# A planned mLSTM and feed-forward kernel: the last 64 rows of w_in in two slices of their own, the gates of chunk 0 in a first small load, and own due times for single jobs

## The chip, the core and the metric

The program runs on one core of a Trainium2 chip. The time is the device time of one execution in microseconds (us). The median of three runs of the kernel before is 493.52 us, the lowest 492.1 and the highest 497.03.

## What is computed

An mLSTM (a recurrent attention with exponential gates) over 4 batches, 8 heads, 768 steps and head width 40, and then a feed-forward layer over all 3072 tokens, all in float32. Cut to what matters:

```python
for t in range(768):
    m_new = maximum(f[t] + m, i[t])
    C = exp(f[t] + m - m_new) * C + exp(i[t] - m_new) * outer(v[t], k[t])
    n = exp(f[t] + m - m_new) * n + exp(i[t] - m_new) * k[t]
    y[t] = sigmoid(o[t]) * (C @ q[t]) / maximum(abs(n @ q[t]), 1)
    m = m_new
x = y as (3072 tokens, 320)
h = x @ w_in                      # 320 x 2048
g = h * clip(h + 3, 0, 6) / 6
out = g @ w_out                   # 2048 x 320
```

## The kernel before

The sequence is cut into chunks of 128 steps. A unit is three chunks of one batch (384 tokens), and there are eight units. Each unit has two tasks (four heads each), so task 2u and 2u+1 belong to unit u; within a task there is one job of each kind per chunk, and names such as `gw2_2` read task 2, chunk 2. `gates` scans the two gates along time on 32 partitions and turns the results into columns by products on the tensor engine (tile `pc`, which needs the loads `img` and `signs`). `gate` makes the decay matrix `gw`: for the first eight by products on the tensor engine (`gb`), later by a broadcast DMA of a scratch array (`gw<-gsc`), a masking instruction on POOL and four exponentials on ACT. `front` multiplies keys and queries (`s`) and DVE multiplies the result into `gw`; `state` and `all_states` make and update the state (`c`, `C`); `back` multiplies by the values (`o`) and gives back the `gw` buffer in the first tasks; `fin` divides, applies the output gate and transposes into `xh` and `xl` (tile `x`).

The feed-forward layer keeps float32 accuracy by splitting each operand into a high and a low part. For block f of 128 of the 2048 hidden columns, `mm1` runs eight products into `h` (L907): three with the first 128 rows of w_in, three with the next 128, and two with the last 64 rows, whose high and low parts lie one above the other in the tile `wtl`. ACT and DVE then make `g` (L921, L923), its high part `gh` (L407) and low part `gl` (L931); `mm2` accumulates three products per block into `acc` (L950 to L952). Two `h` tiles exist, so the third `mm1` of a unit waits until DVE has read the first.

The weights come as raw words that two passes on ACT (L839, L841), two on DVE (L844, L849) and splits (`whi`, `wlo`, `wtl` for w_in; `vh`, `vl` for w_out) turn into these parts. w_in comes in eight slices of 640 words a partition (`weight_slice`, kind `i`: 512 words of the first 256 rows, and 128 of the last 64), w_out in eight of 640. Three `raw` buffers hold them: a load waits until DVE has run L849 on an earlier slice.

Nothing is ordered by the hardware's own choice. A planner in the kernel (`Plan`) takes jobs as generators with due times and estimated costs, and writes one fixed order for PE, ACT, DVE, POOL and the DMA queue of SP. Each engine then works through its row strictly in order, so an instruction that waits holds back all behind it on that engine, and a DMA that waits for its buffer holds back all later DMAs. While the tensor engine has nothing ready in the first unit, the planner sets filler products (`pw`, L428) that keep it active; they end with the first `mm1`. Of 182 fillers, 59 stand ahead of the first product of `gates` and 123 behind it.

## Time and profile before

| | us |
|---|---|
| median of three runs | 493.52 |
| lowest, highest | 492.1, 497.03 |
| the profiled execution, its own time | 497.03 |
| its span, first to last instruction | 495.3 |
| PE busy in the span | 483.8 |
| DVE, ACT, POOL busy | 364.2, 304.9, 43.7 |

The profile shows one execution, the one of 497.03 us; 1.7 us of it lie outside its span. In its rows each line is a group or an instruction with its start, its length and, in square brackets, the idle time of its engine just before it and what ended that. Matmuls overlap their successors, so a group on PE ends about 0.2 us after the next one starts, and the start of the next row is the better mark. PEclk or the clock column is the granted clock of the tensor engine, 1.00 at 2.4 GHz and 0.50 at 1.2 GHz.

### The profile page before, as it was taken

Reading aid. Unit: us, or ns where it says so; the run is one execution under the profiler, and the core shown is the slowest. Engines: PE = TensorE matmul, PEld = TensorE weight load, DVE = VectorE, ACT = ScalarE, POOL = GpSimd, SP = SyncE. Lnnn points to the kernel's source line nnn. Section 1 sums busy time; section 2 is a strip of 40 time slices with the busy share of each in tenths; the row PEclk is TensorE's granted clock in tenths of the full one; section 3 lists DMA queues with packets and bytes.
Section 4 is the critical chain, followed back from the end, with each engine's and each line's share of the span. In section 5 each row is a group of like instructions: output and inputs, shape, how many; then the busy total and the mean of one; then the engine's idle time right before and its main releaser. Section 6 shows DMA issues by size and latency. Waiting matters only on the chain.

```text
span 495.3 us, 10928 instructions
## 1 busy us (share of the span) xinstructions
PE 483.8 (98%) x4222; PEld 465.8 (94%) x4222; DVE 364.2 (74%) x828; ACT 304.9 (62%) x766; POOL 43.7 (9%) x65
## 2 busy tenths in 40 slices
PE   7999998999999999999999999999999999999997
PEld 7899898989999999998899999999999999999997
DVE  4789997999859789597668779688767887534431
ACT  3787997976666657376564656566654755434331
POOL 2012212021210100010010001001010000000000
PEclk9799999999999999999999999999999999999999
DMA  8565948323422323132412423114320110000001
GB/s 269 195 230 197 328 159 299 100 106 119 135 62 65 124 91 106 58 108 80 141 48 66 143 72 119 45 54 156 124 65 22 63 49 15 0 1 26 15 1 41
DMA packets 24676, 50.74 MB, mean 102 GB/s; under 512 B 2576, under 2 KB 9168, under 8 KB 24624
## 3 DMA queue, kind: packets, MB, share of 16 engines
q1 hardware_dynamic: 24624, 50.05, 30.9%
q8 instruction: 33, 0.54, 0.4%
q14 instruction: 19, 0.16, 0.1%
HBM read 46.01 MB, written 4.03 MB: 101 GB/s over the span
## 4 chain that ended last, share of the span: by engine, by line
PE 68%; DVE 12%; DMA 10%; ACT 5%; issue 2%; POOL 2%; SPq 0%; POOLq 0%; DVEq 0%; ACTq 0%
PE h L907 27%; PE acc L950 9%; PE acc L951 8%; PE acc L952 8%; DMA gw<-gsc 7%; PE s L705 4%; PE s L708 2%; ACT gw L678 2%; POOL gw L672 2%; DVE gl L931 2%; PE o L756 2%; DVE g L923 1%; PE c L606 1%; DMA nat<-in_nat_dram 1%; DVE p L738 1%
## 5 line engine op out<-in xcount | busy, mean ns | idle before, releaser
L950 PE MATMUL acc<-vh,gh 128*128 128x320 f32 x384 | 121.0, 315 | 0.0
L951 PE MATMUL acc<-vl,gh 128*128 128x320 f32 x384 | 118.3, 308 | 0.0
L952 PE MATMUL acc<-vh,gl 128*128 128x320 f32 x384 | 118.2, 308 | 0.0
L923 DVE SCALAR_TENSOR_TENSOR g<-g,h 128x384 f32<-128x384 f32 x128 | 67.7, 550 | 55.4 <-ACT g L921 54.5
L907 PE MATMUL h<-xh,whi 128*128 128x384 f32 x256 | 90.8, 355 | 2.4 <-DVE g L923 2.2
L921 ACT ACTIVATE g<-h,half 128x384 f32<-128x384 f32 x128 | 69.9, 575 | 34.1 <-PE h L907 33.4
L907 PE MATMUL h<-xh,wlo 128*128 128x384 f32 x256 | 86.3, 337 | 0.0
L907 PE MATMUL h<-xl,whi 128*128 128x384 f32 x256 | 86.2, 337 | 0.0
L678 ACT ACTIVATE gw<-gw,cT 128x128 f32<-128x128 f32 x160 | 54.1, 397 | 44.4 <-POOL gw L672 44.4
L931 DVE TENSOR_TENSOR gl<-g,gh 128x384 fp32r<-128x384 f32 x128 | 70.7, 567 | 4.8 <-ACT gh L407 3.6
L407 ACT CAST gh<-g 128x384 fp32r<-128x384 f32 x128 | 63.1, 514 | 16.0 <-DVE g L923 15.5
L950 PEld LDWEIGHTS acc<-vh,gh 128*128 128x128 f32 x384 | 72.0, 188 | 0.5
L951 PEld LDWEIGHTS acc<-vl,gh 128*128 128x128 f32 x384 | 72.2, 188 | 0.0
L952 PEld LDWEIGHTS acc<-vh,gl 128*128 128x128 f32 x384 | 72.0, 188 | 0.0
L672 POOL TENSOR_SCALAR_AFFINE_SELECT gw<-gw 128x512 f32<-128x512 f32 x40 | 29.3, 733 | 300.3 <-DMA gw<-gsc 228.9
L907 PEld LDWEIGHTS h<-xh,whi 128*128 128x128 f32 x256 | 48.0, 188 | 5.7 <-DVE g L923 4.1
L907 PEld LDWEIGHTS h<-xh,wlo 128*128 128x128 f32 x256 | 48.0, 188 | 0.3 <-DVE wlo L865 0.3
L907 PEld LDWEIGHTS h<-xl,whi 128*128 128x128 f32 x256 | 48.1, 188 | 0.0
L713 DVE TENSOR_TENSOR gw<-s,gw 128x512 f32<-128x512 f32 x48 | 33.0, 687 | 18.0 <-PE s L708 9.1
L907 PE MATMUL h<-xl,wtl 128*128 128x384 f32 x128 | 43.1, 337 | 0.0
L907 PE MATMUL h<-xh,wtl 128*128 128x384 f32 x128 | 43.1, 337 | 0.0
L722 ACT ACTIVATE ht<-s,eG 128x42 f32<-128x42 f32 x120 | 25.5, 296 | 25.4 <-DVE gw L713 25.4
(97 smaller groups left out, 789.9 us busy)
## 6 DMA issues: line engine op xcount, KB each, us to landing
st<-in_qk_dram SPq DMA_DIRECT2D x48, 256.0 KB, 4.0
gw<-gsc SPq DMA_DIRECT2D x40, 256.0 KB, 3.3
nat<-in_nat_dram SPq DMA_DIRECT2D x16, 492.0 KB, 4.9
rawi<-in_w_in_dram SPq DMA_DIRECT2D x8, 640.0 KB, 6.0
rawo<-in_w_out_dram SPq DMA_DIRECT2D x8, 640.0 KB, 6.0
on<-in_on_dram SPq DMA_DIRECT2D x8, 480.0 KB, 4.5
out_dram<-ob SPq DMA_DIRECT2D x24, 160.0 KB, 2.3
f_s<-in_fg_dram SPq DMA_DIRECT2D x1, 96.0 KB, 4.1
```

Of the source, the lines that this page charges most:

```text
L407: nc.scalar.copy(dst, src)
L672: nc.gpsimd.affine_select(gw, gw, pattern=[[0, 4], [1, L]], compare_op=ALU.is_ge, fill=NEG, base=0, channel_multiplier=-1)
L678: nc.scalar.activation(gw[:, h, :], src[:, h, :], AF.Exp, bias=cT[:, c, r0 + h : r0 + h + 1], scale=1.0)
L713: nc.vector.tensor_tensor(gw.rearrange("p (z j) l -> p z (j l)", z=2), sp[:, :, : 2 * L], gw.rearrange("p (z j) l -> p z (j l)", z=2), ALU ...
L722: nc.scalar.activation(hv[:, z, j], sp[:, z, 2 * L + j * E2 : 2 * L + j * E2 + E2], AF.Copy, scale=eG[:, c, r0 + h : r0 + h + 1])
L907: nc.tensor.matmul(hp, w, x, start=n == 0, stop=n == len(seq) - 1)
L921: nc.scalar.activation(g, hp, AF.Relu, bias=half, scale=1.0 / 6.0)
L923: nc.vector.scalar_tensor_tensor(g, g, 1.0, hp, ALU.min, ALU.mult)
L931: E(e).tensor_sub(gl, g, gh.bitcast(F32))
L950: nc.tensor.matmul(acc, gh[:, ts_], VH[f // 4][:, f % 4, :], start=f == 0, stop=False)
L951: nc.tensor.matmul(acc, gh[:, ts_], VL[p][:, f % 2, :], start=False, stop=False)
L952: nc.tensor.matmul(acc, gl[:, ts_], VH[f // 4][:, f % 4, :], start=False, stop=f == NF - 1)
```

## The change

Four things are changed.

1. w_in comes as eight slices of 512 words (its first 256 rows) and two new slices of kind `t`, of 512 words each, that hold the last 64 rows: half of the 2048 columns in each, on all 128 partitions. A `t` slice takes the same four passes as the others, then two casts and two subtractions of 64 partitions by 512 on ACT or DVE, in place of two casts and two subtractions of 64 by 128 in each of the eight slices. `mm1` for block f waits for `i` slice f//2 and `t` slice f//8.
2. Both gates lie side by side in one input, `figs`. Chunk 0 of both comes in a first load (32 KB), the other five chunks in a second (160 KB); the copy for `img` and the `signs` come by two loads that are a request of their own to the planner.
3. The planner adds a number to the due time of single jobs (`SHIFT`, some 120 entries between -44.6 and +43.2, such as -44.6 for `weight_slice_t_0_0`, -35.9 for `weight_slice_i_7_14`, +24.1 for `weight_slice_i_2_4`).
4. Its other constants are set anew, and so are letters that give passes to engines (`ENGINES`): `ht<-s,eG` is now always on DVE (30 of 40 were on ACT), the first cast of `p` always on ACT and the second on either (56 of 72 casts are on ACT now, 36 before), `weigh` may go to ACT too, and the last subtraction of `vb` and a multiplication of the output gate may go to POOL.

A second way to make `wlo`, by products on PE (`NPE`), is in the code and switched off (`NPE = 0`).

```diff
+NPE = 0
-ENGINES = 'ddpxadxxdaddddddxdaaaaadaaxxy'
+ENGINES = 'dxpxadzxdaadddddxxyaaaadaaxxd'
...
     def add(self, due, gen, after=(), att=1, slack=None, hot=False):
         self.n += 1
+        due += SHIFT.get(name_of(gen), 0.0)
...
         if c0 == 0:
-            yield "q", 200, 1.9
-            nc.sync.dma_start(f_s, fg)
-            nc.sync.dma_start(i_s, ig)
-            nc.sync.dma_start(img[:BH], ig)
+            both = figs.rearrange("p (k t) -> p k t", k=2)
+            yield "q", 200, 0.95
+            nc.sync.dma_start(GT["fi"][mid, :, :L], both[:, :, :L])
+            nc.sync.dma_start(GT["fi"][mid, :, L:], both[:, :, L:])
+            t = plan.now["t"]
+            yield "q", 200, 0.95
+            nc.sync.dma_start(img[:BH], figs[:, S:])
             nc.sync.dma_start(signs, ident_d[:, 128:])
+            event("signs")
+            plan.now["t"] = t
...
         yield "wait", "ident"
+        yield "wait", "signs"
...
+        m = WC if kind == "o" else WI
-        yield "q", 655
-        nc.sync.dma_start(raw.rearrange("p n w -> p (n w)"), (w_in if kind == "i" else w_out)[i].bitcast(U32))
+        yield "q", 1.024 * m
+        nc.sync.dma_start(raw.rearrange("p n w -> p (n w)"), {"i": w_in, "t": w_tail, "o": w_out}[kind][i].bitcast(U32))
...
-            e = yield pick(4, a=0.6, d=Lock(0.55))
-            cast(e, tl[a, 0:128], w[a, 512:640])
-            cast(e, tl[z, 128:256], w[z, 512:640])
-            e = yield pick(5, d=Lock(0.64), g=2 * cg(128))
-            E(e).tensor_sub(tl[z, 0:128], w[a, 512:640], tl[a, 0:128].bitcast(F32))
-            E(e).tensor_sub(tl[a, 128:256], w[z, 512:640], tl[z, 128:256].bitcast(F32))
...
+        elif kind == "t":
+            a, z = slice(0, 64), slice(64, 128)
+            ta, tz = wtl[:, i * 1024 : i * 1024 + WI], wtl[:, i * 1024 + WI : (i + 1) * 1024]
+            for p, o, tl in ((a, z, ta), (z, a, tz)):
+                e = yield pick(4, a=0.18 + 0.00084 * WI, d=lf(WI))
+                cast(e, tl[p], w[p])
+                e = yield pick(5, d=ld(WI), g=cg(WI))
+                E(e).tensor_sub(tl[o], w[p], tl[p].bitcast(F32))
...
     for n in range(WS):
         plan.add(moe_at(0, n / WS) - WAI, weight_slice("i", n, 2 * n))
+        if n % 4 == 0:
+            plan.add(moe_at(0, n / WS) - WAI + WAT, weight_slice("t", n // 4, 2 * n))
```

The order that the planner writes moves at many places. Three of them follow; line numbers of the changed kernel are higher by 10 to 34.

The DMA queue of SP at the start of the program, before (`on` is the output gate, `nat` keys and values, `st` keys and queries, `rawi` a slice of w_in):

```order
L553 DMA on_105<-in_on_dram 128x3x320
L446 DMA f_s<-in_fg_dram 32x768
L447 DMA i_s<-in_ig_dram 32x768
L448 DMA img<-in_ig_dram 32x768
L449 DMA signs<-in_ident_dram 128x192
L436 DMA ident<-in_ident_dram 128x128
L542 DMA nat_106<-in_nat_dram 128x984
L529 DMA st_0_107<-in_qk_dram 128x512
L833 DMA rawi_109<-in_w_in_dram 128x1280
```

The same place in the change (`rawt` is a slice of the last 64 rows):

```order
L447 DMA ident<-in_ident_dram 128x128
L575 DMA on_105<-in_on_dram 128x3x320
L459 DMA fi<-in_figs_dram 32x2x128
L460 DMA fi<-in_figs_dram 32x2x640
L551 DMA st_0_106<-in_qk_dram 128x512
L564 DMA nat_107<-in_nat_dram 128x984
L856 DMA rawt_109<-in_w_tail_dram 128x1024
L463 DMA img<-in_figs_dram 32x768
L464 DMA signs<-in_ident_dram 128x192
```

`signs` moves from fifth to ninth, behind `st`, `nat` and the first `t` slice. On PE the first `s` product now stands ahead of the first product of `gates`; of 173 fillers 107 stand ahead of that product (40 of them behind the `s`), and 66 behind it.

DVE ahead of the last product of unit 0's stretch, the multiplication into `gw2_2`, before (`vr`, `vl` belong to w_out, `yi`, `yo` to the raw passes):

```order
L849 SCALAR_TENSOR_TENSOR vr1_630<-yo1_542,rawo1_481 128x640
L819 TENSOR_TENSOR xl0_529<-x1_1_0_751,xh0_528 128x384
L766 TENSOR_TENSOR ht2_595<-ht2_595,o2_1_770 128x168
L844 TENSOR_SCALAR yi4_627<-yi4_627 128x640
L877 TENSOR_TENSOR vl1_781<-vr1_630,vh0_616 128x640
L713 TENSOR_TENSOR gw2_2_625<-s2_2_771,gw2_2_625 128x512
L819 TENSOR_TENSOR xl0_529<-x2_1_0_786,xh0_528 128x384
```

The same place in the change:

```order
L867 TENSOR_SCALAR yi4_614<-yi4_614 128x512
L841 TENSOR_TENSOR xl0_535<-x1_1_0_735,xh0_534 128x384
L871 SCALAR_TENSOR_TENSOR vr1_757<-yo1_560,rawo1_523 128x640
L735 TENSOR_TENSOR gw2_2_657<-s2_2_746,gw2_2_657 128x512
L788 TENSOR_TENSOR ht2_628<-ht2_628,o2_1_750 128x168
L746 TENSOR_TENSOR ht2_628<-s2_2_746,eG_82 128x168
L911 TENSOR_TENSOR vl1_781<-vr1_757,vh0_607 128x640
L841 TENSOR_TENSOR xl0_535<-x2_1_0_772,xh0_534 128x384
```

The low part of the second slice of w_out (`vl1`) moves from just ahead of that multiplication to behind it. On PE, the `front` products of the next task (`s3_0`) move from behind the first two `mm1` to ahead of them, and the first three `mm1` then follow each other.

ACT around the first `mm1`, before (`g0_0` is the first pass over the first `h`):

```order
L678 ACTIVATE gw3_0_746<-gw3_0_746,cT_81 128x128 x4
L678 ACTIVATE gw3_1_778<-gw3_1_778,cT_81 128x128 x2
L921 ACTIVATE g0_0_879<-h0_0_849,half_80 128x384
L678 ACTIVATE gw3_1_778<-gw3_1_778,cT_81 128x128
L407 CAST vh1_892<-vr2_888 128x640
L921 ACTIVATE g0_1_904<-h0_1_878,half_80 128x384
```

The same place in the change:

```order
L700 ACTIVATE gw3_0_732<-gw3_0_732,cT_81 128x128 x4
L417 CAST whi_75<-yi4_614 128x2x256
L862 ACTIVATE yi5_794<-rawi5_782 128x512
L864 ACTIVATE rawi5_782<-rawi5_782 128x512
L955 ACTIVATE g0_0_864<-h0_0_840,half_80 128x384
L577 ACTIVATE on1_800<-on1_800 128x3x320
L955 ACTIVATE g0_1_882<-h0_1_863,half_80 128x384
```

The two passes over the raw words of w_in slice 5 now stand ahead of `g0_0`, and the output gate of unit 1 ahead of `g0_1`. The load of slice 5 waits for the buffer that `vr1` (the DVE rows above) gives back.

## Rows read from the trace of the kernel before

**Rows 1.** From the page: the span, the busy time of each engine, and the clock of the tensor engine in 40 slices of the span.

```profile
span 495.3 us, 10928 instructions
PE 483.8 (98%) x4222; PEld 465.8 (94%) x4222; DVE 364.2 (74%) x828; ACT 304.9 (62%) x766; POOL 43.7 (9%) x65
PEclk9799999999999999999999999999999999999999
```

**Rows 2.** The timeline of PE from 0 to 62 us: start, length, instruction, and in brackets the idle time before it.

```profile
1.06 5.37 PE L428 MATMUL pw<-ones 128*128 128x128 bf16 x59 [1.06 <-POOL ones L421]
7.97 0.49 PE L491 MATMUL pc<-signs,img 96*128 96x128 f32 x2 [1.55 <-DVE img L472]
...
9.42 0.71 PE L705 MATMUL s<-st 64*128 64x128 f32 x8 [0.23 <-DMA st<-in_qk_dram]
10.07 0.34 PE L428 MATMUL pw<-ones 128*128 128x128 bf16 x3
...
16.06 0.44 PE L606 MATMUL c<-vp,nat 128*64 128x42 f32 x8 [0.26 <-ACT gw L678]
...
17.86 0.44 PE L606 MATMUL c<-vp,nat 128*64 128x42 f32 x8 [0.34 <-DVE C L409]
...
41.41 1.12 PE L428 MATMUL pw<-ones 128*128 128x128 bf16 x17
...
43.09 1.63 PE L428 MATMUL pw<-ones 128*128 128x128 bf16 x26
...
52.23 1.09 PE L756 MATMUL o<-nat,gw 128*128 128x42 f32 x8 [0.94 <-DVE gw L713]
53.15 0.42 PE L907 MATMUL h<-xh,whi 128*128 128x384 f32 x1
```

**Rows 3.** Stretches of 2 us from 8 to 18 us: us, busy time of PE, weight loads, DVE, ACT and POOL with their instructions, the granted clock, the share of the DMA engines, and GB/s.

```profile
8.00:10.00 2.00, 1.77 (x22) 1.54 (x22) 1.87 (x5) 0.52 (x4) 0.00 (x0) 1.00 0.98 379
...
14.00:16.00 2.00, 1.80 (x18) 1.59 (x16) 1.89 (x6) 1.47 (x8) 0.08 (x1) 1.00 0.94 370
16.00:18.00 2.00, 1.60 (x21) 1.46 (x23) 1.94 (x7) 1.96 (x9) 0.00 (x0) 1.00 0.10 38
```

**Rows 4.** One wider stretch, all engines in the same columns.

```profile
18.50:25.50 7.00, 7.00 (x54) 6.43 (x54) 3.87 (x13) 4.09 (x11) 0.00 (x0) 0.52 0.39 131
```

**Rows 5.** Waits of PE from 53 to 120 us: total, times, longest.

```profile
PE h L907 <- DVE g L923: 2.0, 2, 1.4
```

**Rows 6.** The same from 120 us to the end.

```profile
PE o L758 <- DVE C L619: 0.8, 2, 0.5
PE o L761 <- DVE p L738: 0.5, 1, 0.5
PE o L760 <- ACT p L407: 0.3, 1, 0.3
PE h L907 <- DVE g L923: 0.2, 1, 0.2
```

**Rows 7.** The DMA queue of SP at the start: start, length of the issue, tile.

```profile
3.05 0.42 SPq L449 DMA_DIRECT2D signs<-in_ident_dram  x1
...
5.12 0.86 SPq L833 DMA_DIRECT2D rawi<-in_w_in_dram  x2
```

**Rows 8.** The timeline of ACT: the instruction that waited for the first slice of w_in.

```profile
11.00 0.79 ACT L839 ACTIVATE yi<-rawi 128x640 f32<-128x640 f32 x1 [1.07 <-DMA rawi<-in_w_in_dram]
```

**Rows 9.** The chain of waits of the whole program, around the first `mm1`: start, length, what the end waited for.

```profile
40.49 5.72 DMA gw<-gsc
...
46.36 0.64 POOL gw L672
...
47.03 0.69 ACT gw L678 x2
...
50.31 1.04 issue
...
51.50 0.69 DVE gw L713
52.23 1.09 PE o L756 x8
53.32 2.86 PE h L907 x16
```

**Rows 10.** The timeline of DVE: one instruction of the same stretch.

```profile
50.27 1.30 DVE L877 TENSOR_TENSOR vl<-vr,vh 128x640 fp32r<-128x640 f32 x1
```

**Rows 11.** The view of the tile `rawi`: time from issue to landing of its eight loads.

```profile
DMA to landing us min/median/max: 3.8/6.0/9.3
```

**Rows 12.** Groups of ACT instructions from 53 to 120 us: count, busy us, mean ns of one, and the idle time before them.

```profile
L722 ACT ACTIVATE ht<-s,eG 128x42 f32<-128x42 f32 x17 | 3.7, 298 | 0.4 <-DVE gw L713 0.4
L407 ACT CAST whi<-yi 128x512 fp32r<-128x512 f32 x4 | 2.5, 620 | 0.0
...
L407 ACT CAST wtl<-yi 64x128 fp32r<-64x128 f32 x8 | 2.4, 297 | 0.1
L841 ACT ACTIVATE rawi<-rawi 128x640 uint32<-128x640 uint32 x3 | 2.4, 791 | 0.0
```

**Rows 13.** From the page, the costliest groups: the passes that turn `h` into `g`, with count, busy us, mean ns of one, and the idle time of the engine before them.

```profile
L923 DVE SCALAR_TENSOR_TENSOR g<-g,h 128x384 f32<-128x384 f32 x128 | 67.7, 550 | 55.4 <-ACT g L921 54.5
...
L921 ACT ACTIVATE g<-h,half 128x384 f32<-128x384 f32 x128 | 69.9, 575 | 34.1 <-PE h L907 33.4
```

**Rows 14.** One stretch later on, in the columns of rows 3.

```profile
80.00:100.00 20.00, 18.59 (x158) 17.43 (x157) 17.70 (x40) 19.54 (x42) 1.56 (x4) 1.00 0.58 202
```

More of the change, by code (lines that the diff above doesn't have):

```diff
@@ L25 @@
 WC = 640
+WI = 512
+WAT = 14.426
 NEG = -1.0e30
@@ L49 @@
 NRAW = 3
-SPAN = 85.078
-T0 = 227.472
-AH = 11.606
+SPAN = 82.689
+T0 = 235.691
+AH = 6.112
 GP = [1, 2, 1, 2]
-G0 = -164.7
-G1 = 19.632
-G2 = 100.338
-AH1 = 3.428
+G0 = -140.122
+G1 = 29.702
+G2 = 118.356
+AH1 = 8.351
 FC = 0
 FCS = {2: [[(0, 2)], [(0, 1), (1, 1)]], 3: [[(0, 3)], [(0, 2), (2, 1)], [(0, 1), (1, 1), (2, 1)], [(0, 1), (1, 2)]], 1: [[(0, 1)], [(0, 1)]]}
-LON = -24.316
-WAI = -16.391
-WAO = -37.306
-WAS = 137.753
-MV = -2.634
-DELTA = -1.049
+LON = -28.143
+WAI = -13.123
+WAO = -40.095
+WAS = 109.704
+MV = -2.298
+DELTA = -1.405
 EGW = 1
-EV = 80.942
-EG = -23.479
+EV = 102.156
+EG = -38.496
 HOP = 0.167
@@ L82 @@
 RATE_D = 300.0
-BL = 3.335
+BL = 2.337
 T_WARM = 6.9
 WGAP = 0.055
-ENGINES = 'ddpxadxxdaddddddxdaaaaadaaxxy'
-BG = -0.356
-BA = -1.135
-BD = -0.41
+ENGINES = 'dxpxadzxdaadddddxxyaaaadaaxxd'
+BG = -0.283
+BA = -0.362
+BD = -0.296
 GS = 6
 FD = 2
-FIN0 = -213.18
+FIN0 = -202.157
 NE = 0
@@ L148, in mat, with name_of @@
     return m
+def name_of(gen):
+    code, given = gen.gi_code, gen.gi_frame.f_locals
+    return "_".join([gen.__name__] + [str(given[v]) for v in code.co_varnames[: code.co_argcount]])
 class Plan:
@@ L349, in mlstm_moe_kernel @@
 @with_exitstack
-def mlstm_moe_kernel(ctx: ExitStack, tc: tile.TileContext, ig, fg, qkd, natd, ond, w_in, w_out, ident_d, out):
+def mlstm_moe_kernel(ctx: ExitStack, tc: tile.TileContext, figs, qkd, natd, ond, w_in, w_tail, w_out, ident_d, out):
     nc = tc.nc
@@ L430, in mlstm_moe_kernel @@
     GT = {k: early["ea"].tile(sh, F32, name=k) for k, sh in dict(
-        f_s=[64, S], i_s=[64, S], lf=[64, S], img=[128, S], signs=[128, 192], one=[64, L], sel=[128, 8, L]).items()}
+        fi=[64, 2, S], lf=[64, S], img=[128, S], signs=[128, 192], one=[64, L], sel=[128, 8, L]).items()}
     GT.update({k: early["ea"].tile([128, L], BF16, name=k) for k in ("mask", "identb")})
+    GT["nident"] = early["ea"].tile([128, L], F32R, name="nident")
     def load_ident():
@@ L851, in weight_slice @@
         if kind == "i":
-            hi, lo, tl = whi[:, :, fs], wlo[:, :, fs], wtl[:, fs]
-            wm = w[:, 0:512].rearrange("p (a f) -> p a f", a=2)
-            a, z = slice(0, 64), slice(64, 128)
+            fs = slice(i * 256, (i + 1) * 256)
+            hi, lo = whi[:, :, fs], wlo[:, :, fs]
+            wm = w.rearrange("p (a f) -> p a f", a=2)
             e = yield pcast(24, 512)
             cast(e, hi, wm)
-            plan.now["t"] -= ca(512)
-            e = yield pick(4, a=0.6, d=Lock(0.55))
-            cast(e, tl[a, 0:128], w[a, 512:640])
-            cast(e, tl[z, 128:256], w[z, 512:640])
-            e = yield pick(5, d=Lock(0.64), g=2 * cg(128))
-            E(e).tensor_sub(tl[z, 0:128], w[a, 512:640], tl[a, 0:128].bitcast(F32))
-            E(e).tensor_sub(tl[a, 128:256], w[z, 512:640], tl[z, 128:256].bitcast(F32))
-            e = yield psub(7, 512)
-            E(e).tensor_sub(lo, wm, hi.bitcast(F32))
+            if i < NPE:
+                yield "wait", "nident"
+                gb = yield ("get",) + banks(0, "o")
+                pb = bank(gb, [128, 2, 256], f"wl{i}")
+                yield "p", mat(1, 512, 4) + mat(1, 512)
+                nc.tensor.matmul(pb, ident, wm, start=True, stop=False)
+                nc.tensor.matmul(pb, GT["nident"], hi, start=False, stop=True)
+                yield "a", ca(512)
+                nc.scalar.copy(lo, pb)
+                put(*gb)
+            else:
+                e = yield psub(7, 512)
+                E(e).tensor_sub(lo, wm, hi.bitcast(F32))
+        elif kind == "t":
[6 more added lines that the diff above has]
+                E(e).tensor_sub(tl[o], w[p], tl[p].bitcast(F32))
         put(*gy)
@@ L997, in mlstm_moe_kernel @@
         if quad == 0:
[L998 removed]
+            plan.add(max(due(u, k - 1 + LON), -98.0), load_on(u), (), 1, sl)
         before = {cp: "{}_{}".format(*order[rank[task, cp] - 1]) if rank[task, cp] else None for cp in range(n)}
@@ L1040, in mlstm_moe_kernel @@
             plan.add(0, release(rel_vp), states)
-    plan.add(0, release(open_moe), [f"gw{t}_{x}" for t, x in order[2 * UNITS[0] : GB]] + [f"fin1_{UNITS[0]-1}", f"state0_{UNITS[0]-1}", f"state1_{UNITS[0]-1}"])
+    plan.add(0, release(open_moe), [f"gw{t}_{x}" for t, x in order[2 * UNITS[0] : GB]] + [f"wi{n}" for n in range(NPE)] + [f"fin1_{UNITS[0]-1}", f"state0_{UNITS[0]-1}", f"state1_{UNITS[0]-1}"])
     for n in range(WS):
         plan.add(moe_at(0, n / WS) - WAI, weight_slice("i", n, 2 * n))
+        if n % 4 == 0:
+            plan.add(moe_at(0, n / WS) - WAI + WAT, weight_slice("t", n // 4, 2 * n))
         plan.add(moe_at(0, n / WS) - WAO + SPAN / 16, weight_slice("o", n, 2 * n + 1))
@@ L1048, in mlstm_moe_kernel @@
             pre = [f"m1_{u}_{f-1}"] if f else [f"m1_{u-1}_{NF-1}"] * (u > 0)
-            plan.add(moe_at(u, f / NF) - MV, mm1(u, f), pre + [f"wi{f//2}", f"fin{2*u+1}_{UNITS[u]-1}", "mo"], 0)
+            plan.add(moe_at(u, f / NF) - MV, mm1(u, f), pre + [f"wi{f//2}", f"wt{f//8}", f"fin{2*u+1}_{UNITS[u]-1}", "mo"], 0)
         for p in range(NF // 2):
@@ L1056, in mlstm_moe_kernel @@
         plan.run()
-_INS = ["ig", "fg", "qk", "nat", "on", "w_in", "w_out", "ident"]
+_INS = ["figs", "qk", "nat", "on", "w_in", "w_tail", "w_out", "ident"]
 _OUTS = [((B * S, DM), "float32")]
```

41 lines of the change are left out of this document (22 added, 19 removed).

## The prediction

> **What bounds the kernel now.** I began with busy times. The tensor engine is busy for 483.8 of 495.3 us at nearly full clock throughout; DVE and ACT have a quarter and a third of the span to spare [rows 1]. The change takes no real product away and adds none, so it can alter only four things: when the first real product starts, how many fillers stand among the real ones, how long PE waits, and at which clock the real ones run.
>
> The second view was the timeline of PE up to the first `mm1`, which starts at 53.15 us [rows 2]. Ahead of the first product of `gates` at 7.97 us stand 59 fillers and a wait of 1.55 us for a scan on DVE. Behind it, four waits add up to 0.23 + 0.26 + 0.34 + 0.94 = 1.77 us, and 123 fillers lie between the real products. The third view was the clock by stretches: it is full up to 18 us and half from about 18.5 to 25.5 us [rows 3, 4]. Seven us at half clock cost some 3.4 us of the tensor engine's time (7.00 busy us at 0.52: 7.00 x 0.48). The fourth was the list of waits after 53 us: 2.0 us up to 120 us [rows 5], 0.8 + 0.5 + 0.3 + 0.2 = 1.8 us later [rows 6], some 3.8 us in all. So all that the change can win back is in the first 53 us, bar those 3.8 us.
>
> The profiled execution took 497.03 us, the longest of the three shown; the median is 493.52, 3.5 us below it. That is about the price of the half-clock stretch. I read the other runs as having less of it, which no row shows.
>
> **The start.** `signs` was issued at 3.05 us as the fifth load [rows 7]; now it is the ninth, and the first product of `gates` needs it. The ninth load of before is the first slice of w_in, issued at 5.12 us; ACT waited for it until 11.00 us [rows 7, 8]. Nine loads then carried 480 + 4 x 96 + 64 + 492 + 256 + 640 = 2316 KB (the sizes of the tiles in the order). Now they carry 64 + 480 + 32 + 160 + 256 + 492 + 512 + 96 + 96 = 2188 KB. The queue moved 370 to 379 GB/s in those stretches [rows 3], so 128 KB less is some 0.35 us: a landing at about 10.6 us, against 7.97 us for the product before. That is +2.6 us. One real group, `s` of chunk 0, which took 10.07 - 9.42 = 0.65 us [rows 2], now runs in that time. Net **+2.0 us**; bounds +1.4 (the 40 fillers behind that `s` end by about 10.0 us, and the load is no later) and +3.0 (landing a us later). The smaller first gate load, which lets the scan start earlier, gains nothing here: the scan is no longer what ends last. It only brings the scans of later chunks forward.
>
> **The fillers.** Behind the first gate product stand 66 in place of 123. One costs (1.63 - 1.12) / (26 - 17) = 0.057 us at full clock [rows 2]. 57 fewer are **-3.2 us**, if real products are ready in their place; if not, each turns into a wait and the gain is nothing.
>
> **The waits up to the first mm1s.** The stretch behind `o1_2` (40.4 us) is set by a chain: the `gw` load of 5.72 us, the mask, the exponentials, a multiplication on DVE at 51.50 us [rows 9]. In that chain DVE lost time to `vl1`, which took 1.30 us [rows 10] after waiting for ACT and now stands behind the multiplication. So about 1.3 us of chain go, and the PE work behind `o1_2` is about as long as the chain that is left; I expect some 0.7 us of wait there, as against 0.94. A second wait is likely early on: DVE now does the `t` slice among the scans before the first `gw` is multiplied, some 0.8 us for `o0_0`. The third is new. On ACT the two passes over slice 5 now stand ahead of `g0_0`, and the third `mm1` can't start before DVE has finished `g0_0`. Their load waits for a buffer that DVE gives back just ahead of the multiplication into `gw2_2`. From there to the first `mm1` go that multiplication (0.69 [rows 9]), `o2_2` (53.15 - 52.23 = 0.92 [rows 2]) and `s3_0` (about 1.0 by its place in the order: the `s` of 0.65 and a smaller one), 2.6 us. A load takes at least 3.8 us [rows 11], 0.35 less for 128 KB, so it lands 0.85 us behind the start of the first `mm1`. Two passes of about 0.63 us (0.791 x 512/640 [rows 12]) and `g0_0` on ACT and DVE (0.575 + 0.55 [rows 13]) end at 3.25 us, 3.9 with the DVE passes of slices 2 and 5 in between; the first two `mm1` cover 2.86 [rows 9]. That leaves about 1.1 us of wait. In sum 0.8 + 0.7 + 1.1 = 2.6 us in place of 1.77: **+0.8 us**. Bounds: -1.8 (nothing waits) and +6.3 (that load takes 9.3 us, the longest of rows 11, so 5.5 more than the shortest).
>
> **The clock.** The fall at about 18.5 us came after 14 to 18 us with PE busy for 1.80 + 1.60 of 4 us, and with no single wait over 0.34 us since 9.5 us [rows 2, 3]. In the change the same small products (`c`, `o`, `pc`) stand in that stretch, with the wait for `o0_0`. I therefore leave the clock as it was, 0.0 us, with bounds -3.4 (no such stretch) and +3.4 (a second one). The Trainium skill, TensorE: Matmul & The Clock Gate, section on HAM oscillation, has the clock fall when the engine idles long between bursts, as in a wait for a DMA. By it this stretch should not have come at all, and the sum would be 3.4 us lower for both kernels; the rows disagree, so I don't use it. The next section of that page, on a second failure mode, lets short idle times between groups of matmuls do the same, and that is what the rows look like.
>
> **After 53 us.** The 2.0 us up to 120 us are two waits of `mm1` for DVE's `g` [rows 5], which takes its input from ACT; ACT was busy for 19.54 of 20 us from 80 to 100 us [rows 14]. ACT loses work there. `ht<-s,eG`, 3.7 us up to 120 us [rows 12], goes to DVE. The 16 tail casts of 0.297 us (4.8 us over the kernel) become four of 64 x 512, which I price by the nearest row, the 0.620 us of `whi` [rows 12]: 2.5 us. The 16 raw passes of 640 words (12.7 us) become 20 of 512 at the 0.63 us above (12.6). To ACT come 20 casts of `p`, most of them later on. I take 1.5 of the 2.0 us away and leave the 1.8 us behind them, where ACT and DVE have room: **-1.5 us**, between -2.5 and +3 (an order in which other waits come up). The two more DMAs on SP cost it about 0.43 us of issue each, in a queue that is seldom full; POOL takes five passes (of `p`, `vb` and the output gate) and gives up two `wlo` and three of `weigh`: nothing, since no wait of rows 5 and 6 ends on it. The end of the program is the same, row by row.
>
> **Sum.** 2.0 - 3.2 + 0.8 + 0.0 - 1.5 = -1.9 us against the profiled 497.03, that is 495.1 with a half-clock stretch, and 491.7 without. From the median 493.52 it is 491.6. I forecast **491.6 us**, 0.4% less; a difference under 1% (4.9 us) is about what a measurement of this kernel can't tell from no change.
>
> **Rivals.**
> - *The load of slice 5 holds ACT* (slower). Place: ACT ahead of `g0_0`. For it: strict order, and a queue in which such loads took 6.0 us in the median and up to 9.3 [rows 11]. Against it: at this moment only small loads are ahead of it. It decides from a landing of about 7 us on; at 9.3 us it adds 5.5: 497.1 us. If it also pushes the passes of the following slices, another 2 us.
> - *The fillers turn into waits*. The chain of rows 9 is fixed by a load and by DVE, and fewer fillers don't shorten it. Then the 3.2 us don't come: 494.8 us. For it: the wait of 0.94 us that was there in spite of the fillers. Against it: DVE has about 3 us less to do on the way, without `vl1` and with shorter passes.
> - *The half clock doesn't come back*. If the median of before still holds its 3.4 us and the denser products keep the clock up, the time is 488.2 us. For it: 107 fillers up to 10 us and gate products right behind. Against it: the stretch of small products is there as before, and I think the median holds little of it.
> - *DVE is the new bound* from 53 to 120 us, since it takes over `ht`: 17 more passes there at about 0.3 us would only cost where DVE is late, some 3 us: 496 us.
>
> **Chances.** My forecast 0.50 (own range 489 to 494.5); slice 5 0.12; fillers to waits 0.15; clock 0.17; DVE 0.06. The range takes in the filler and the clock case in the main and reaches into the slow ones: **487.5 to 496.8**. More than 1% faster means below 488.6: most of the clock case and a little of the forecast, 0.20. More than 1% slower means above 498.5: a part of slice 5 and DVE, 0.06. Within: 0.74.
>
> **What would show it.** Right: the first gate product at about 10.6 us, waiting for `signs`; the first `mm1` at 48 to 50 us without half clock (51 to 53 with it), `s3_0` ahead of it; a wait of about 1 us before the third `mm1`, ended by DVE `g`; waits of `mm1` between 60 and 120 us of about half a us. Wrong: a first gate product at 9 us or 12 us; a wait of several us behind the second `mm1`, with ACT idle for a `rawi` load; waits in place of the fillers; a half-clock stretch that moved or doubled; new waits of `mm1` for DVE in 60 to 120 us.

## The result: half a per cent slower, and the profile after

The changed kernel takes 496.83 us in the median of 20 executions (493.3 to 500.68), the kernel before 494.27 us in 20 beside it. The ratio is 1.0056 with a 95% interval of 1.0029 to 1.0082: slower, by less than the 1% that I had set as the bound of a difference, but clear of noise. I had forecast 491.6 us and a small gain; 496.83 lies just above the upper end of my range. Twelve more executions, taken later, gave the ratio 1.0061 (1.0027 to 1.0095).

The profiled execution took 496.37 us, 0.66 us *less* than the one of before. A single trace of each would have named the wrong winner: the four traces of the kernel before that there are in the end show executions of 497.03, 495.83, 495.87 and 493.93 us, all above the median of its later executions, 493.32 us. So the runs are read by their means too, and by a second number that comes with every execution: its **clock loss**, (1 - mean granted clock) x span. The clock is on record to 0.001, so the loss of one execution is known in steps of some 0.5 us.

Of 146 later executions of the kernel before (beside the experiments) the mean is 493.49 us and the mean clock loss 1.05 us; of 32 of the changed one 496.71 and 2.53. By this account almost half of the 3.2 us between them is clock; the section on why the prediction was wrong shows that this is too much. Executions more than 1.5% longer than the fastest of the same kernel beside them are left out here and below, nine of the kernel before (one of 1613.51 us; with the other eight, of 497.17 to 500.66 us, its mean is 493.78 us and its clock loss 1.21) and one each of head2 and b_natlate.

The page of the changed kernel: busy times, and the clock in 40 slices [rows 1].

```profile
span 494.4 us, 10823 instructions
PE 482.6 (98%) x4213; PEld 463.8 (94%) x4213; DVE 360.5 (73%) x828; ACT 293.8 (59%) x666; POOL 44.8 (9%) x65
PEclk9999899999999999999999999999999999999999
```

The timeline of PE from 9 to 24 us (start, length, instruction, in brackets the idle time before it and what ended it), which answers to [rows 2]:

```profile
12.19 0.46 PE L513 MATMUL pc<-signs,img 96*128 96x128 f32 x2 [0.98 <-DMA signs<-in_ident_dram]
...
19.02 0.44 PE L628 MATMUL c<-vp,nat 128*64 128x42 f32 x8 [0.89 <-ACT gw L700]
19.82 1.06 PE L778 MATMUL o<-nat,gw 128*128 128x42 f32 x8 [0.36 <-DVE gw L735]
```

And from 49 to 68 us:

```profile
50.42 0.45 PE L941 MATMUL h<-xh,whi 128*128 128x384 f32 x1
...
53.81 0.44 PE L941 MATMUL h<-xh,whi 128*128 128x384 f32 x1 [0.35 <-DVE g L957]
54.09 0.34 PE L941 MATMUL h<-xl,whi 128*128 128x384 f32 x1
...
56.84 1.14 PE L778 MATMUL o<-nat,gw 128*128 128x42 f32 x8 [1.37 <-DMA nat<-in_nat_dram]
57.78 0.67 PE L941 MATMUL h<-xh,whi 128*128 128x384 f32 x1
58.25 0.52 PE L941 MATMUL h<-xl,whi 128*128 128x384 f32 x1
```

The first gate product waits for `signs`, as forecast, but at 12.19 us. Up to 12 us the queue had moved some 2.94 MB (245 GB/s x 12 us, first row below), 0.7 MB more than the nine loads hold (2188 KB, 2.24 MB): it was already carrying loads that were issued behind `signs`. The first `mm1` starts at 50.42 us, with `s3_0` ahead of it, and the third waits only 0.35 us. What I hadn't forecast stands at 56.84 us: `o3_0`, now right behind the third `mm1`, waits 1.37 us for the load of `nat`, and the matmuls behind it take 0.52 us in place of 0.34. The clock of the stretches explains the longer matmuls (us, busy time of PE, weight loads, DVE, ACT, POOL with their instructions, granted clock, DMA share, GB/s; as [rows 3, 4]):

```profile
0.00:12.00 12.00, 9.53 (x115) 9.06 (x115) 4.68 (x14) 2.77 (x3) 3.63 (x10) 1.00 0.75 245
...
18.00:21.00 3.00, 1.76 (x21) 1.53 (x19) 2.81 (x9) 2.77 (x11) 0.00 (x0) 1.00 0.63 249
21.00:28.00 7.00, 7.00 (x100) 6.36 (x98) 6.51 (x16) 6.35 (x17) 0.58 (x1) 1.00 0.52 158
...
50.00:57.60 7.60, 5.89 (x41) 5.23 (x40) 5.99 (x14) 6.42 (x15) 0.63 (x1) 1.00 0.91 278
57.60:61.20 3.60, 3.60 (x24) 3.16 (x24) 2.30 (x4) 2.30 (x6) 0.75 (x1) 0.53 1.01 406
```

The half clock of before at 18.5 us is missing in this execution, and a shorter one stands behind the wait for `nat`. The waits of PE (total, times, longest) from 50 to 125 us, which answer to [rows 5], and then from 120 us to the end [rows 6]:

```profile
PE h L941 <- DVE g L957: 1.8, 3, 0.8
PE o L778 <- DMA nat<-in_nat_dram: 1.4, 1, 1.4
```

```profile
PE h L941 <- DVE g L957: 0.6, 2, 0.4
PE o L780 <- DVE xl L841: 0.4, 1, 0.4
PE x L835 <- DVE xl L841: 0.2, 1, 0.2
```

### The profile page after: what moved, and what is told of

Its sections match the earlier page's. It is cut to its first block, busy times and chain, and to the rows that moved or that the text cites. A ratio compares the mean times of both kernels' runs of the same rounds, so it can differ in the third digit from the quotient of the medians.

```text
span 494.4 us, 10823 instructions
## 1 busy us (share of the span) xinstructions
PE 482.6 (98%) x4213; PEld 463.8 (94%) x4213; DVE 360.5 (73%) x828; ACT 293.8 (59%) x666; POOL 44.8 (9%) x65
## 4 chain that ended last, share of the span: by engine, by line
PE 78%; DMA 9%; DVE 7%; ACT 2%; issue 1%; POOL 1%; SPq 1%; POOLq 0%; DVEq 0%; ACTq 0%
PE h L941 32%; PE acc L984 10%; PE acc L985 9%; PE acc L986 9%; PE s L727 5%; DMA gw<-gsc 4%; DMA nat<-in_nat_dram 3%; PE s L730 2%; PE o L778 2%; PE c L628 2%; DMA signs<-in_ident_dram 1%; PE x L835 1%; DVE g L957 1%; ACT gw L700 1%; POOL gw L694 1%
## 5 line engine op out<-in xcount | busy, mean ns | idle before, releaser
L955 ACT ACTIVATE g<-h,half 128x384 f32<-128x384 f32 x128 | 71.0, 574 | 47.9 <-PE h L941 45.2
L417 ACT CAST p<-gw 128x512 bf16<-128x512 f32 x56 | 34.6, 617 | 32.6 <-DVE gw L735 29.4
L941 PE MATMUL h<-xh,wtl 128*128 128x384 f32 x128 | 43.2, 338 | 0.0
```

Of the source, the lines that this page charges most:

```text
L417: nc.scalar.copy(dst, src)
L941: nc.tensor.matmul(hp, w, x, start=n == 0, stop=n == len(seq) - 1)
L955: nc.scalar.activation(g, hp, AF.Relu, bias=half, scale=1.0 / 6.0)
```

## The experiments

A summary first: median, ratio to the kernel before on the same chip with its 95% interval, the mean with the mean clock loss (us) of the same executions, and both for the kernel before beside them. The kernel before itself has means of 493.14 to 493.99 us and clock losses of 0.66 to 1.43 us from chip to chip, so a mean is best held against the last column. The ratio of the changed kernel is that of its first 20 executions, its last column belongs to the other 12.

| kernel | n | median | ratio | mean | clock loss | before: mean, clock loss |
|---|---|---|---|---|---|---|
| before | 146 | 493.32 | 1 | 493.49 | 1.05 |  |
| changed | 32 | 496.83 | 1.0056 (1.0029 to 1.0082) | 496.71 | 2.53 | 493.14, 0.87 |
| o3_swap | 12 | 497.40 | 1.0091 (1.0059 to 1.0123) | 497.79 | 2.57 | 493.14, 0.87 |
| head_early | 12 | 498.53 | 1.0106 (1.0074 to 1.0138) | 498.40 | 3.73 | 493.14, 0.87 |
| calm | 12 | 496.20 | 1.0051 (1.0018 to 1.0084) | 496.01 | 1.69 | 493.63, 1.28 |
| nostand | 12 | 494.95 | 1.0064 (1.0030 to 1.0098) | 495.90 | 1.98 | 493.17, 0.66 |
| light | 12 | 497.05 | 1.0080 (1.0045 to 1.0115) | 497.00 | 3.14 | 493.17, 0.66 |
| noshift | 10 | 493.15 | 1.0001 (0.9970 to 1.0033) | 493.52 | 0.69 | 493.17, 0.66 |
| noshift_again | 12 | 493.74 | 1.0009 (0.9979 to 1.0040) | 494.03 | 1.32 | 493.75, 1.10 |
| s_head | 11 | 498.33 | 1.0103 (1.0069 to 1.0137) | 498.46 | 1.86 | 493.38, 1.04 |
| s_tail | 12 | 495.23 | 1.0036 (1.0010 to 1.0063) | 495.17 | 1.15 | 493.38, 1.04 |
| fill | 12 | 496.27 | 1.0049 (1.0020 to 1.0077) | 496.19 | 1.07 | 493.99, 1.43 |
| nostand_fill | 12 | 494.60 | 1.0006 (0.9980 to 1.0031) | 494.58 | 0.29 | 493.99, 1.43 |
| head2 | 11 | 496.80 | 1.0062 (1.0024 to 1.0100) | 497.20 | 3.29 | 493.38, 1.04 |
| b_natlate | 11 | 496.77 | 1.0057 (1.0018 to 1.0096) | 496.29 | 2.16 | 493.63, 1.28 |
| b_fill | 12 | 491.42 | 0.9955 (0.9925 to 0.9985) | 491.65 | 0.20 | 493.75, 1.10 |

### Both kernels once more

> The changed kernel once more, with a second trace. Theory nat (the second wait-and-clock loss of the changed trace is systematic): the wait of PE for the load of nat at about 56.8 us comes again, 1 us or more, and half clock behind it, 1 to 2 us of loss. Theory clock (half-clock stretches fall anywhere, by chance): the stretch stands elsewhere or is missing, and the nat wait may shrink. Both: ratio to the kernel before 1.003 to 1.008.

> The kernel before once more, for a second trace. If its half-clock stretch at 18.5 to 25.5 us belongs to the order of its work, it is there again (span about 495); if it is chance, it is missing, PE is at full clock up to 53 us, the first mm1 starts at about 49.8 us and the span is about 492.

The wait for `nat` came again (1.60 us), with half clock behind it, and another half-clock stretch at 40 us:

```profile
39.70:43.30 3.60, 3.60 (x31) 3.20 (x31) 2.00 (x8) 2.66 (x8) 0.00 (x0) 0.53 0.69 226
...
60.00:64.00 4.00, 4.00 (x29) 3.48 (x28) 2.67 (x8) 2.78 (x7) 0.64 (x1) 0.57 1.02 407
```

In the kernel before the stretch at 18.5 us was chance: its second and third traces have full clock there, and half clock from about 51 to 55 us, behind a wait for `o2_2` of 1.55 and 1.31 us.

> The kernel before, a third trace. In most executions its clock is full; then the first mm1 stands at about 49.5 us. Theory bound: with the clock loss gone the waits for DVE g at 84 and 105 us are longer than 2.0 us together. Theory nat: they are 1 to 2 us as in the other two traces, and the span is about 491.

> The kernel before, a fourth trace, in the hope of one near its median (493.3 us) rather than 2 to 4 us above it as the three so far. Theory head: it differs from them ahead of the first mm1, by shorter waits for the chain behind the load of gw. Theory later: it differs between 53 and 120 us.

The third trace, around that wait:

```profile
48.00:52.00 4.00, 2.69 (x28) 2.52 (x26) 3.82 (x7) 3.35 (x11) 1.15 (x2) 1.00 0.74 287
52.00:55.60 3.60, 3.60 (x15) 3.19 (x13) 2.58 (x4) 2.20 (x6) 0.56 (x1) 0.53 1.03 350
```

The fourth, at full clock throughout, waited 1.63 us at the same place and took 493.93 us. So the three have full clock up to about their first `mm1`, and these are its starts in b_again, b_third and b_fourth:

```profile
51.58 0.67 PE L907 MATMUL h<-xh,whi 128*128 128x384 f32 x1
51.05 0.42 PE L907 MATMUL h<-xh,whi 128*128 128x384 f32 x1
51.23 0.42 PE L907 MATMUL h<-xh,whi 128*128 128x384 f32 x1
```

In the first trace, with the half clock at 18.5 us, it was 53.15 us [rows 2]. The stretch had cost 1.6 to 2.1 us there, and not the 3.4 us that it took from PE: without it PE waits longer, for `o2_2` above all, 1.31 to 1.63 us in place of 0.94. There is no trace of the kernel before in an execution of 490 to 492 us, so where the kernel before gains in its quick executions stays unseen.

### One wait taken away, by hand

Here, and in the runs that follow except those with another table of due times, the order of all other instructions is kept: the edit holds back single instructions and writes them later, leaves some out or adds fillers.

PE's order in o3_swap against the change (`o3_0` is `back` of task 3 and chunk 0, `h0_3` the fourth `mm1`; `g0_3` below is its pass `g`, `gh0_3` the cast of that):

```diff
 h0_2
-o3_0
 h0_3
+o3_0
```

> The changed kernel with one edit: the eight products of o3_0 stand behind the fourth mm1 instead of ahead of it, so that the load of nat has 1.4 us more to land. Theory nat: the wait of 1.37 us goes and with it the half clock behind it: 1.4 to 3.0 us less than the changed kernel, ratio to before 0.998 to 1.002. Theory head (the loss lies in the later start of the gate products): 0 to -1.4 us, half clock unchanged, ratio about 1.003 to 1.005. Theory clock: no gain beyond 1.4 us, ratio about 1.003.

The wait for `nat` went, and another took its place: the fourth `mm1` itself waits, since ACT stands on the load of `on` ahead of the pass `g` of the second. The ratio, 1.0091, is no better than that of the change. Waits of PE from 50 to 65 us:

```profile
PE h L947 <- DVE g L965: 1.7, 2, 1.4
PE c L629 <- DVE ht L794: 0.4, 1, 0.4
```

So calm moves this pass too; ACT's order against o3_swap:

```diff
-tanh of on1
 g0_1
...
 g0_2
+tanh of on1
```

> The changed kernel with two passes moved: o3_0 on PE behind the fourth mm1 (as in the run before), and on ACT the tanh of the second unit's output gate behind the pass g of the third mm1, so that ACT no longer stands on the load of `on` at 53 to 54 us and g0_1 comes 1.5 us earlier. Theory nat (the waits at 54 to 58 us are the loss): both waits go, PE starts the fourth mm1 right behind the third, lateness at that place 1.5 to 1.9 us less; ratio to before 0.998 to 1.002. Theory bound (from 53 to 110 us the passes on ACT and DVE set the pace, so a wait taken away there comes back as waits of mm1 for DVE g by 110 us): the waits go but others come, ratio 1.004 to 1.007.

Both waits are gone, and the ratio, 1.0051, is within the noise of the 1.0056 and 1.0061 of the change. What DVE stands on (50 to 62 us) suggests why no more came of it: DVE itself needs that load, for `vp`.

```profile
DVE vp L598 <- DMA nat<-in_nat_dram: 1.2, 1, 1.2
DVE ht L796 <- PE o L781: 0.6, 1, 0.6
```

### DVE as the bound?

In the changed kernel DVE waits for `nat` a second time (its timeline at 88 us):

```profile
88.19 0.33 DVE L595 TENSOR_TENSOR vp<-nat,wT 128x168 f32<-128x168 f32 x1 [1.71 <-DMA nat<-in_nat_dram]
```

Since DVE is busy for 54.6 of the 60 us from 60 to 120 (55.8 in the kernel before, so no more than there), I took it for the bound, as in one of my rivals, and tried this from two sides: nostand takes its stands away, light its work. The orders of SP, DVE and ACT in nostand, one after the other, against calm (vp4 and vb4 belong to task 4):

```diff
-load of on1
 load of gw
 load of nat3
+load of on1
...
-vp4, one pass
 g0_10
 g0_11
+vp4, one pass
...
-vb4, first cast
 gh0_10
+vb4, first cast
```

And light against the change:

```diff
+LEFT = {5, 7, 8, 9, 10, 11, 12, 13, 14, 15}
...
-        E(e).tensor_scalar(w, w, W_MAX, -W_MAX * W_SIGN, ALU.min, ALU.max)
+        if n not in LEFT:
+            E(e).tensor_scalar(w, w, W_MAX, -W_MAX * W_SIGN, ALU.min, ALU.max)
```

> The changed kernel with the two passes moved as in calm, and three moves that keep DVE and ACT from standing on loads of nat: the load of `on` behind the nat load issued at 49.5 us (nat lands 1.3 us earlier), and for the nat load that lands at 88 us one pass vp of DVE behind the next two passes g, one cast vb of ACT behind the next cast gh. Nothing is added or left out. Theory DVE (from 53 to 118 us DVE is the bound in both kernels, and the changed one is late because DVE stands some 2.5 us longer, on nat loads above all): DVE's idle time from g of the first mm1 to g of the twentieth falls from 6 to 3 or 4 us, 2 to 3 us less than the changed kernel, ratio 0.998 to 1.002. Theory spread (the loss is many small waits all along): no more than 1 us, ratio 1.003 to 1.006.

> The changed kernel without the clamp of the weight words (the DVE pass min/max) in ten slices whose clamp falls between 50 and 112 us, and in one before: 4.5 us of DVE work less in that stretch; the computation is changed by that, as infinite or overflowing words are no longer clamped. Theory DVE: what DVE no longer does there comes off the end nearly whole, 3 to 4.5 us less than the changed kernel, ratio 0.996 to 1.000. Theory spread, or one in which PE or the loads set the pace: at most 1.5 us, ratio 1.003 to 1.006.

light refutes it: 4.5 us less to do on DVE, and the time is that of the changed kernel (497.05 and 496.83 us in the median). nostand's mean is 0.8 us less, its ratio no better. In the other direction, a wait put into the kernel before does cost it. SP's order in b_natlate:

```diff
-load of nat3
 load of rawo
+load of nat3
```

> The kernel before with one edit: the nat load that was issued at 53.7 us is issued behind the rawo load that followed it, 640 KB later. o3_0 at 60.9 us then waits some 1.5 us for it. Theory nat: the kernel before becomes slower by this wait and by half clock behind it in some executions, 1.5 to 3 us, ratio 1.003 to 1.006. Theory bound: waits of mm1 for DVE g at 84 and 105 us shrink by as much, ratio 0.999 to 1.002.

The ratio is 1.0057, by a delay that in the profiled execution held DVE for 1.0 us and PE for 0.5:

```profile
DVE vp L576 <- DMA nat<-in_nat_dram: 1.0, 1, 1.0
```

That execution itself took only 492.20 us, so its trace doesn't show where the others lose. In the mean it is 2.7 us slower than the kernel before beside it, of which 0.9 is clock loss (2.16 and 1.28 us).

### Which part of the change

> The changed kernel with an empty table of own due times: loads, slices, engines and constants of the change stay, the order is the planner's without it. If the own due times carry the loss (they put the nat loads late), it is as fast as the kernel before, ratio 0.997 to 1.002. If the two other parts carry it (nine loads ahead of the gate product, slices of w_in in 10 loads), it is slower still, 1.005 to 1.02.

> The changed kernel with an empty table of own due times once more, beside b_fill, with five rounds in place of three. If the own due times carry the whole loss: ratio 0.998 to 1.002 again, clock loss below 1 us in the mean. If the first result was chance: 1.003 or more.

```diff
-SHIFT = {'weight_slice_i_7_14': -35.9, 'gate_2_0': -12.6,
...
+SHIFT = {}
```

Without the own due times (the table has 110) the changed kernel equals the one before, twice, within 0.3 to 0.4%. The tail slices, the gate loads, the engines and the constants cost nothing together that these runs can tell; **the own due times carry the loss**. One half of the second expectation failed: the clock loss was 1.32 us and not below 1. In noshift the gate loads come first, and the first gate product starts at 10.14 us with `s0_0` and one filler ahead of it.

> The changed kernel with the own due times of the jobs of the first unit up to the first mm1 alone (45 of 110); the loads of the start, the late signs and the early tail slice stay as in the change. Theory head (the late gate product and the early tail slice cost 1.5 to 2.5 us and draw half clock at 14 to 28 us): slow as the whole change, ratio 1.004 to 1.009. Theory later (the order of mm1 and of the second unit costs it): ratio 0.997 to 1.002.

> The other 65 own due times alone: those of the second unit, of the mm1 and mm2 of the first, of the later slices. The head is that of noshift, with the first gate product at about 10 us. Theory head: ratio 0.996 to 1.002, half clock in few executions. Theory later: ratio 1.004 to 1.009, with the waits for nat at 55 and 86 us there.

Each half alone loses too (1.0103 and 1.0036), and the two don't add up to the 1.0056 of both. So I read the loss as one of the order that comes out, and not of one job's due time. Most of it isn't clock: in the mean s_head is 5.1 us slower than before beside it with 0.8 us more clock loss, s_tail 1.8 us slower with 0.1 more.

### The head put right by hand

The orders of SP, ACT and PE in head_early against the change:

```diff
 small load of fi
+load of img
+load of signs
 big load of fi
...
-load of img
-load of signs
...
+identb
 tanh of on0
 yt, first pass
-identb
...
 s0_0
-28 fillers
 12 fillers
 first gate product
```

> The changed kernel with the loads of the gates' image and of signs issued right behind the small gate load, the cast of the identity first on ACT, and 28 of the 40 fillers ahead of the first gate product left out. Both loads land by about 6.5 us in place of 12; the first gate product starts at about 9.6 us in place of 12.2. Theory head: what follows moves up with it by 1.5 to 2.5 us, ratio to before 0.999 to 1.002. Theory nat or clock: the chain of exponentials and scans behind it eats most of it as waits, gain 0 to 0.7 us, ratio 1.004 to 1.006.

The gate product starts 2.7 us earlier, and the gain turns into waits: 1.73 us for `st` ahead of `s0_0`, where fillers stood, and others behind it, on ACT, which stands on the load of the tail slice ahead of the exponentials (timeline of PE from 8 to 21 us):

```profile
8.13 0.72 PE L729 MATMUL s<-st 64*128 64x128 f32 x8 [1.73 <-DMA st<-in_qk_dram]
...
9.46 0.44 PE L514 MATMUL pc<-signs,img 96*128 96x128 f32 x2
...
13.36 0.38 PE L688 MATMUL gb<-mask,identb 128*128 128x512 bf16 x1 [1.29 <-ACT dec L529]
...
15.38 0.49 PE L514 MATMUL pc<-signs,img 96*128 96x128 f32 x2 [0.76 <-ACT dec L529]
```

It is *slower* than the change: on the same chip 498.40 us in the mean in place of 496.51, with a clock loss of 3.73 us in place of 2.02. In the profiled executions PE is busy for 7.84 us from 10 to 21 us, 8.78 in the change, and the clock then falls:

```profile
14.00:21.00 7.00, 5.13 (x53) 4.63 (x52) 6.56 (x17) 5.89 (x23) 0.11 (x1) 1.00 0.59 204
21.00:28.10 7.10, 7.10 (x59) 6.41 (x58) 4.59 (x13) 3.72 (x10) 0.00 (x0) 0.52 0.40 118
```

> The changed kernel with its head put right by hand: as head_early, and the two ACT passes and two DVE passes on the first tail slice behind the exponentials of chunk 0, so that ACT doesn't stand on its load from 6.4 to 11.5 us. The first gate product at about 9.6 us and no wait of 1 us or more behind it; lateness of PE at 20 to 40 us some 2 us less than in the changed kernel. Theory head: this stays to the end, half clock gets rarer, ratio 0.998 to 1.003. Theory later: it is given back by 110 us, ratio 1.004 to 1.007.

head2 also has the passes on the tail slice behind the exponentials of chunk 0, so that ACT doesn't stand. It gave 1.0062 (1.0024 to 1.0100) with a clock loss of 3.3 us, and it missed what it was for. In the one trace the first gate product starts at 12.10 us, as late as in the change: `s0_0` ahead of it waits 2.25 us for `st`, and the clock is half behind that. There are still 1.26 us of wait at 17.6 us and 0.83 at 20.9.

```profile
9.69 1.22 PE L735 MATMUL s<-st 64*128 64x128 f32 x8 [2.25 <-DMA st<-in_qk_dram]
...
12.10 0.74 PE L516 MATMUL pc<-signs,img 96*128 96x128 f32 x2
```

So neither run shows an early gate product without waits around it. head_early shows that an earlier start with the idle time left in is no gain.

### Fillers in the waits

So the waits stay where they are, and are filled: `more(n)` writes n more fillers ahead of a product that waits anyway.

```diff
         yield "p", mat(4 * n, 128, 1, 96, 128)
+        if c0 == 0:
+            more(18)
...
             yield "p", KV
+            if (task, cp) == (0, 0):
+                more(16)
             outer(task, cp, cps)
...
+        if (task, cp) == (0, 0):
+            more(6)
```

> The changed kernel with 40 more fillers, put into three waits of PE that each trace of it shows: 18 ahead of the first gate product (12.2 us), 16 ahead of the first product of the state (19.0 us), 6 ahead of o0_0 (19.8 us). At 0.057 us each they fit into the waits of 0.98, 0.89 and 0.36 us. Theory clock (idle PE at 10 to 20 us draws the half clock that follows at 21 to 29 us, and with fewer fillers the change has more such executions): mean clock loss falls from 2.5 us to 1.5 or less, ratio 1.002 to 1.004. Rival (the clock falls whatever stands in those waits): loss stays 2 to 3.5 us, ratio 1.005 to 1.008.

> nostand with the same 40 fillers. Theory clock and stands together: the clock loss of 1.98 us falls to 1 or less, executions at full clock stay at about 493.9 us; mean 494.5 to 495, ratio 1.001 to 1.004. Rival: as nostand, mean 495.9, ratio 1.004 to 1.008.

Stretches of fill; the second pair is its wait for `nat`, 2.69 us long in this execution:

```profile
12.00:21.00 9.00, 8.88 (x98) 8.36 (x96) 8.09 (x20) 6.86 (x29) 0.47 (x1) 1.00 0.71 257
21.00:28.50 7.50, 7.50 (x104) 6.86 (x104) 6.97 (x18) 6.50 (x17) 0.92 (x1) 1.00 0.51 162
55.50:58.40 2.90, 0.21 (x3) 0.04 (x1) 0.21 (x2) 2.10 (x7) 0.63 (x1) 1.00 1.03 333
59.70:63.30 3.60, 3.60 (x25) 3.08 (x25) 2.10 (x7) 2.26 (x7) 0.64 (x1) 0.53 1.00 401
```

and of nostand_fill, where neither place idles for long:

```profile
12.00:21.00 9.00, 8.59 (x94) 8.29 (x95) 7.88 (x20) 7.02 (x29) 0.55 (x1) 1.00 0.71 257
21.00:28.50 7.50, 7.50 (x104) 6.86 (x104) 6.97 (x18) 6.53 (x17) 0.90 (x1) 1.00 0.54 156
52.00:62.00 10.00, 8.84 (x66) 8.35 (x65) 8.13 (x24) 8.82 (x21) 1.58 (x2) 1.00 0.94 353
```

Of the changed kernel's executions 21 of 32 lost 1 us or more to the clock, of nostand's 7 of 12, of fill's 5 of 12, of nostand_fill's 1 of 12; of the kernel before on the chip of the last two, 15 of 22. The mean falls from 496.71 to 494.58 us, by 2.1 us, about as much as the clock loss (2.53 - 0.29), but the chips differ. On one chip, nostand_fill is 1.6 us below fill in the mean, with 0.8 us less clock loss. Its ratio, 1.0006, is that of no difference, where fill alone (1.0049) and nostand alone (1.0064) were slower: it took both the fillers and the moved loads (the intervals of fill and nostand_fill still overlap). And fill is slower than the kernel before beside it although its clock loss is the smaller one, 1.07 as against 1.43 us.

The same for the kernel before, 43 fillers in its four waits, which beats both:

```diff
+18 fillers
 first gate product
...
+4 fillers
 c0_0
...
+5 fillers
 c0_1
...
+16 fillers
 o2_2
```

> The kernel before with 43 more fillers in its own four waits of PE ahead of the first mm1 (18 ahead of the first gate product, 4 and 5 ahead of two products of the state at 16 and 18 us, 16 ahead of o2_2 at 50 us), 0.057 us each. Theory clock: its clock loss of 1.23 us in the mean falls to 0.5 or less, mean 492.4 to 493.2 in place of 493.8, ratio 0.996 to 0.999; then it beats both kernels. Rival (half clock of the kernel before falls for other reasons): loss stays above 1 us, ratio 0.999 to 1.002.

It takes 491.42 us, 0.45% less than before (0.15 to 0.75%), and 1 of 12 executions lost 1 us to the clock, as against 62 of 146. Its page, and PE's timeline at the place of the old wait:

```profile
span 488.0 us, 11014 instructions
PE 482.2 (99%) x4265; PEld 466.0 (95%) x4265; DVE 362.4 (74%) x828; ACT 306.3 (63%) x766; POOL 44.0 (9%) x65
```

```profile
48.28 1.06 PE L426 MATMUL pw<-ones 128*128 128x128 bf16 x16
49.17 1.04 PE L767 MATMUL o<-nat,gw 128*128 128x42 f32 x8
50.03 0.42 PE L918 MATMUL h<-xh,whi 128*128 128x384 f32 x1
```

The mean falls by 2.1 us against the kernel before on the same chip, the clock loss by 0.9; the rest I can't place for certain. In this execution of 489.75 us PE's waits of 0.2 us or more from 50 us to the end are 0.5 us in all, in the four traces of the kernel before 4.4 to 4.7. But those four are longer executions than its median.

## Why the prediction was wrong

By its own steps:

- **The start, +2.0 us: mis-sized.** The mechanism held (`signs` as ninth load holds the first gate product), but it landed later than my 10.6 us: +4.22 us (12.19 - 7.97) less the 0.65 of `s`, so +3.6, outside my bound of +3.0. I counted only the bytes of the nine loads; the queue carried 0.7 MB of others by then.
- **The fillers, -3.2 us: as forecast.** 66 behind the gate product, and real products took their place, so the rival "fillers turn into waits" didn't occur.
- **The waits up to the first `mm1`s, +0.8 us: near.** 0.89 + 0.36 before the first `mm1`, none behind `o1_2`, and 0.35 at the third, 1.6 us in place of my 2.6 and of the 1.77 of before. Slice 5, my slow rival, cost 0.35 us and not 1.1 or more.
- **The start, the fillers and the waits together: about right.** I expected the first `mm1` 1.5 us earlier (2.0 - 3.2 + 1.5 - 1.77). It now starts at 50.42 us, and `s3_0`, which moved ahead of it, takes 1.0 of this. The three traces of before with full clock up to about there have 51.05 to 51.58 us, so it is 1.6 to 2.2 us earlier. With the first term 1.6 us too small, that the sum fits is in part luck. What was wrong is the price of the half clock at 18.5 us: it took 3.4 us from PE, but 1.6 to 2.1 from the start of the first `mm1`.
- **After 53 us, -1.5 us: this step failed.** I priced ACT's passes and left out that `o3_0` moved up to the third `mm1` while its load of `nat` stood behind `on`, `gw` and a slice. The waits from the third `mm1` to 125 us are 2.8 us besides the 0.35 above, as against 2.0, and not 0.5. From the first `mm1` to the last instruction the changed kernel needs 444.0 us (494.4 - 50.42), 442.3 without the 1.7 us of half clock in it, 443.3 with the 1.0 us of `s3_0` that now stands ahead. The four traces of before, counted in the same way, need 440.8 to 442.2. That is 1.1 to 2.5 us more, where I had forecast 0.4 less (-1.5 and the 1.1 at the third `mm1`). The order showed the move of `o3_0`; I asked of two loads only, `signs` and slice 5, when they land.
- **The clock, 0.0 us: this failed too.** I took the stretch at 18.5 us for a property of the order, "left as it was". It is one outcome among several, whose odds the change moves: a mean loss of 2.53 us in place of 1.05 (2.02 and 0.87 on one chip), 1.2 to 1.5 us more, within my bound of +3.4. But it isn't the larger part of what the change costs. The executions at a mean clock of 0.999 or more have a mean of 495.05 us in the changed kernel (11 of 32) and 492.45 in the one before (84 of 146), 2.6 us apart; and those of the changed kernel that lost clock lost 3.8 us of it on average, but are only 2.5 us longer than those that didn't.
- **The rival on DVE** named the right size (496 us) for a wrong reason: light took 4.5 us of work from DVE and gained nothing. Its sum holds only if the 1.5 us of the step above go as well (491.6 + 1.5 + 3), which it doesn't say.

What stays open: with its waits filled and the stands gone the changed kernel is level with before by its ratio, but its executions at a mean clock of 0.999 or more have a mean of 494.29 us (11 of nostand_fill), those of before 492.45 (84). Some 1.8 us remain, which the traces don't settle, as none of before is of a quick execution. The nearest hint is the waits of `mm1` for DVE's `g` from 50 us to the end, in nostand_fill and then in b_fourth, both at full clock:

```profile
PE h L972 <- DVE g L992: 5.0, 8, 0.9
PE h L907 <- DVE g L923: 1.6, 4, 0.6
```

But the first is an execution of 496.29 us, the second longest of twelve, so that this is the cause is not shown.
